# A retention layer and a feed-forward block on one core: five plain and three seven-product pairs in the first pass

## The chip, the cores and the metric

The kernel runs on one core of one Trainium2 chip. TensorE (PE) multiplies 128x128 weights with up to 512 columns; VectorE (DVE), ScalarE (ACT) and GpSimd (POOL) work on tiles of 128 partitions; SyncE (SP) issues all DMAs, in the order in which they are written. Each engine takes its own instructions in order and waits at semaphores for the others. The metric is the time of one execution on the device in microseconds.

## What is computed

```python
scores = (q @ k.T) / sqrt(64)                 # 8 batches, 8 heads, 576 tokens, 64 wide
ret = scores * where(i >= j, gamma[h] ** (i - j), 0)
x = (ret @ v)                                 # to 4608 tokens x 512
h = x @ w_in                                  # 512 x 2048
g = max(h, 0) + log1p(exp(-abs(h)))           # softplus
out = g @ w_out                               # 2048 x 512, fp32
```

The attention is computed in chunks of 128 tokens with a running state for each head. The feed-forward block takes most of the time.

## The kernel before

Every fp32 operand of the feed-forward block is split into a head (rounded to the matmul's fp32r) and a rest, and each product is the sum of three: rest x head, head x rest, head x head (`TERMS`). The tokens are nine units of 512; the hidden layer has 16 blocks of 128, two to a pair J (0 to 7).

Unit 0 goes through alone while the weights are loaded and split. The first pass does units 1 and 2. The three later passes do two units each, with seven products for each pair in both layers (`full_pair`, `full_phase`).

In the first pass most pairs are plain. A plain slot (`plain_slot`) makes one hidden block of one unit: two products of 6 matmuls into one bank (`acc` and `third` in turn), softplus (`size_of`, `log_of` on ACT; L486 on DVE), the split into head (ACT L490) and rest (DVE L494), and the 12 matmuls (L501) of the second layer for the block of the slot before. A slot's `jobs` are written behind that. The last pairs of the pass are made by `strassen_pair`: the four hidden blocks of a pair J, two of each unit, come from seven products in place of eight: B11, B21, T1, T2, B22, T3, NT4, in this order, into the banks `acc`, `two` and `third`. Their partial sums go to four quarters of two `quad` tiles: ACT copies a bank, DVE adds the next to it (L998, L1022, L1028). T2 adds to the bank from which ACT copies c[0] (L996), NT4 to the one that L1028 reads. Output matmuls of the pair before are spread between the products in quarters. The blocks of unit 2 are stored to DRAM (`kept_dram`) and fetched at the end of the pass (`kept_parts`).

A pair's seven products need sums of blocks: of the tokens (T1, T2, T3, NT4; `combined_x`, four subtractions for 128 tokens on POOL, then `finish_combined`: an ACT cast and a DVE subtraction) and of the weights. One set of weights' sums for one J is: whole (head + rest, two DVE additions, L634 or L649), four sums (L659 to L662), two heads (ACT L666), two rests (DVE L670), two stores of 512 KB. Input sums are for the pair's own seven products, output sums for the second layer in the later passes. Before, pairs are plain for J = 0 to 5 (`PLAIN = 6`); output set 0 is made in unit 1's slots, 1 and 2 in the two seven-product pairs, 3 and 4 in unit 2's slots, 5 to 7 in the next pass.

The order on each engine is the order of the code: nothing is moved afterwards. The table `jobs` says behind which slot a piece of work stands, `queued` is a list of DMA issues of which `product` takes one (two, where more than seven wait) behind each weight load. Weight blocks come through a ring of seven tiles, loaded seven products ahead. `quad` tiles are nine, in turn. An attention group (`chunk_products`) of one chunk stands in every second slot and in each seven-product pair, 13 in the first pass; its results leave the banks `two` and `third` through DVE (L244, L430, then the states L272, L273, L282 or L280).

Of the kernel before, what the change touches and what calls it, by code (L numbers as in the profile page):

```python
# [20 lines left out]
C = 128  # L21
NCHUNK = NTOK // C
NPAIR = H // 2
T = 512
# [31 lines left out]
PLAIN = 6  # L56
# [28 lines left out]
def retention_softplus_ffn(ctx: ExitStack, tc, first, whole, others, consts, w, out):  # L85
# [836 lines left out]
    def prepare_rest(j):  # L922
        combine_rest(raws[j])
# [25 lines left out]

    def start_combined(i, engine=nc.gpsimd):  # L950
        tmps[i] = quad().rearrange("p n (a b c) -> p (n a) b c", a=2, b=2)
        combined_x(tmps[i], column(i), engine)
# [4 lines left out]
    def schedule(*rows):  # L957
        plan = {}
        for p, f, *args in rows:
            plan.setdefault(p, []).append(lambda f=f, args=args: f(*args))  # L960
        return plan

    def half_b22(i):
# [5 lines left out]
        (1, prepare, PLAIN + 1), (1, prepare_whole, PLAIN), (2, prepare_sums, PLAIN), (3, prepare_split, PLAIN),  # L969
        (3, half_b22, 0), (4, prepare_store, PLAIN), (4, prepare_whole, PLAIN + 1), (4, prepare_sums, PLAIN + 1),  # L970
        (5, finish_combined, 0, nc.vector), (5, half_b22, 1), (6, prepare_split, PLAIN + 1),
        (6, prepare_ring, 4, 0, 3, 2), (7, prepare_store, PLAIN + 1), (7, prepare_ring, 4, 3, 4, 3),
        (7, finish_combined, 1, nc.vector), (7, half_b22, 2), (8, prepare_sums, 4), (9, prepare_ring, 5),
        (9, finish_combined, 2, nc.vector), (10, prepare_split, 4), (10, prepare_sums, 5), (10, half_b22, 3),
        (11, prepare_store, 4), (11, finish_combined, 3, nc.vector), (11, prepare_head, 5),
        (0, whole_out, 0), (1, combine_out, 0), (2, split_out, 0), (3, store_out, 0),
        *[(5 + 2 * j, raw_store, j) for j in range(4)])
    starts = schedule(*[(3 + 2 * i, start_combined, i) for i in range(CPU)])
    for p in range(2 * PLAIN):
        group = groups.pop() if p % 2 == 0 and p < 10 else None  # L980
        plain_slot(1, p, B11, B21, rest, group, (), *(x.get(p, ()) for x in (jobs, starts)))
# [6 lines left out]
    def strassen_pair(s, J, group, rest, last=False, extra=None):  # L988
# [12 lines left out]
        if extra is not None:  # L1001
            whole_out(extra)
        for j in stores:
            prepare_rest(j)
        if last:
            half_x(B12, STAGE[0, 1], slice(0, T), nc.gpsimd)
        ab = None if J == PLAIN else logs(c[0])
        output_some(-(-len(outputs) // 4))
        while stores:
            prepare_store(stores.pop(0))  # L1010
        product(z, T1, True)
        nc.scalar.copy(c[1], z)  # L1012
        ab = ab or logs(c[0])
        softplus(c[0], ab)
        if extra is not None:
            combine_out(extra)
        product(acc, T2)
        nc.scalar.copy(c[2], acc)
        if extra is not None:
            combine_head(raws["out", extra])  # L1020
# [10 lines left out]
        if extra is not None:  # L1031
            combine_rest(raws["out", extra])
# [33 lines left out]
        return [split_last, lambda: softplus_rest(gs[u1, 2 * J + 1], ab4)], kept  # L1066

    stores = [5]
# [7 lines left out]
    extras = {(0, NJ - 2): 1, (0, NJ - 1): 2}  # L1076
    for s in range(FULL):
        u2 = 2 + 2 * s
        first = PLAIN if s == 0 else 0
        more = s + 1 < NSUPER  # L1080
        for J in range(first, NJ):
            rest, kept = strassen_pair(s, J, groups.pop() if groups else None, rest, s == 0 and J == NJ - 1,
                                       extras.get((s, J)))
# [10 lines left out]
        if first:  # L1094
            blocks = schedule((0, prepare_ring, 0))
            plan = schedule(
                *[(2 * j - 1, prepare_ring, j) for j in range(1, 4)], *[(2 * j, prepare_sums, j) for j in range(4)],
                *[(2 * j + 1, prepare_split, j) for j in range(4)], *[(2 * j + 2, prepare_store, j) for j in range(4)],
                *[(8 + 2 * i, finish_combined, i, nc.vector) for i in range(2)],
                (9, half_x, B21, STAGE[1, 0], whole, nc.vector), *[(2 * j - 7, raw_store, j) for j in range(4, NJ)],  # L1100
                (4, whole_in, 3, 0), (6, combine_out, 3), (7, split_out, 3), (8, store_out, 3),
                (8, whole_in, 4, 1), (9, combine_out, 4), (10, split_out, 4), (11, store_out, 4))
            starts = schedule(*[(min(6 + 2 * i, 2 * first - 1), start_combined, i) for i in range(CPU)])
# [10 lines left out]
            job((0, 0), finish_combined, 2, nc.vector)  # L1114
            job((0, 1), half_x, B11, STAGE[0, 0], whole, nc.vector)
            job((1, 0), finish_combined, 3, nc.vector)
            job((1, 1), half_x, B22, STAGE[1, 1], whole, nc.vector)
# [302 lines left out]
```

## Time and profile before

| | us |
|---|---|
| median of 3 runs | 829.91 (829.48 to 829.99) |
| the profiled execution | 828.55 |
| its span, first to last instruction | 826.8 |
| PE busy | 814.9 (99%) |
| DVE busy | 642.9 (78%) |
| ACT busy | 546.7 (66%) |
| POOL busy | 165.7 (20%) |

A row of the timeline gives when an instruction (or several that follow each other) starts, how long it takes, its engine, line and tiles, and in brackets how long the engine stood idle before it and what released it. PE's matmuls overlap, so what a product takes is read from one start to the next. DVE's operations overlap a little, too: two of 512 columns that are shown as 1.28 us start 0.60 apart.

### The profile page before, as it was taken

How to read it: one execution, taken by the hardware profiler on the slowest of the kernel's cores; microseconds unless marked ns; L12 is line 12 of the kernel's file. 1: busy time of each engine (PE TensorE's matmuls, PEld its weight loads, DVE VectorE, ACT ScalarE, POOL GpSimd, SP SyncE). 2: the span in 40 equal slices, each digit the busy share in tenths (PEclk: the TensorE clock that was granted, in tenths of full speed). 3: DMA queues.
4: the chain of work that ended last, by engine and by line, in shares of the span. 5: the costliest groups of instructions: out<-in, count | busy, mean ns of one | idle time of the engine just before them, and what ended most of it. 6: DMA issues, size and time to landing. Idle time of an engine off the chain costs nothing.

```text
span 826.8 us, 19153 instructions
## 1 busy us (share of the span) xinstructions
PE 814.9 (99%) x7366; PEld 666.3 (81%) x7366; DVE 642.9 (78%) x1068; ACT 546.7 (66%) x957; POOL 165.7 (20%) x228
## 2 busy tenths in 40 slices
PE   8999999999999999999999999999999999999998
PEld 6788888888778888888887888888878888888886
DVE  5899987778787885778989995767889956555875
ACT  5787765546764554677877565776775658878643
POOL 3312221440221453111113000112110002212100
PEclk9999999999999999999999999999999999999999
DMA  9888979887789985598888678878757676666675
GB/s 355 315 296 293 321 238 368 291 290 256 260 288 354 314 301 171 198 304 267 276 259 283 218 213 258 256 226 267 227 166 215 216 245 192 193 194 192 191 216 173
DMA packets 149260, 209.95 MB, mean 254 GB/s; under 512 B 10801, under 2 KB 114737, under 8 KB 149169
## 3 DMA queue, kind: packets, MB, share of 16 engines
q1 hardware_dynamic: 149168, 208.72, 76.5%
q8 instruction: 59, 0.97, 0.5%
q14 instruction: 33, 0.26, 0.1%
HBM read 166.74 MB, written 41.94 MB: 252 GB/s over the span
## 4 chain that ended last, share of the span: by engine, by line
PE 88%; DVE 5%; ACT 4%; DMA 1%; issue 1%; SPq 0%; DVEq 0%; ACTq 0%
PE acc L855 20%; PE sum L1159 19%; PE y L501 14%; PE third L855 11%; PE two L855 4%; PE h L467 4%; PE two L1159 3%; PE acc L1159 2%; PE third L1159 2%; PE third L226 2%; PE two L288 1%; PE two L210 1%; PE two L300 1%; ACT ab L478 1%; ACT ab L479 1%
## 5 line engine op out<-in xcount | busy, mean ns | idle before, releaser
L855 PE MATMUL acc<-xt,ring 128*128 128x512 f32 x768 | 193.7, 390 | 0.9 <-DVE quad L1028 0.6
L1159 PE MATMUL sum<-parts,ring 128*128 128x512 f32 x720 | 174.0, 392 | 0.0
L855 PEld LDWEIGHTS acc<-xt,ring 128*128 128x128 f32 x768 | 143.5, 188 | 32.8 <-DVE quad L1028 1.0
L1149 ACT CAST parts<-g 128x512 fp32r<-128x512 f32 x168 | 102.8, 621 | 88.1 <-DVE g L1169 29.9
L1159 PEld LDWEIGHTS sum<-parts,ring 128*128 128x128 f32 x720 | 133.8, 188 | 28.6 <-DVE parts L1153 0.3
L1153 DVE TENSOR_TENSOR parts<-g,parts 128x512 fp32r<-128x512 f32 x168 | 118.0, 724 | 38.1 <-ACT parts L1149 36.1
L501 PE MATMUL y<-wout,g 128*128 128x512 f32 x576 | 140.1, 392 | 0.3 <-DVE g L494 0.3
L501 PEld LDWEIGHTS y<-wout,g 128*128 128x128 f32 x576 | 107.1, 188 | 23.3 <-PE h L467 0.7
L855 PE MATMUL third<-xt,ring 128*128 128x512 f32 x444 | 111.2, 390 | 0.0
L855 PEld LDWEIGHTS third<-xt,ring 128*128 128x128 f32 x444 | 83.2, 188 | 17.8 <-ACT quad L1012 0.3
L479 ACT ACTIVATE ab<-ab 128x512 f32<-128x512 f32 x120 | 75.9, 632 | 3.8
L478 ACT ACTIVATE ab<-ab 128x512 f32<-128x512 f32 x120 | 75.9, 633 | 3.5
L1169 DVE SCALAR_TENSOR_TENSOR g<-g,ab 128x512 f32<-128x512 f32 x96 | 67.1, 711 | 7.7 <-ACT ab L479 7.5
L203 POOL TENSOR_TENSOR qv<-qv,consts_sb 128x256 f32<-128x256 f32 x61 | 46.3, 758 | 106.2 <-DMA qv<-others 104.9
L490 ACT CAST g<-ab 128x512 fp32r<-128x512 f32 x44 | 27.3, 621 | 45.3 <-DVE ab L486 23.4
L467 PE MATMUL h<-xt,win 128*128 128x512 f32 x192 | 47.3, 395 | 1.1 <-DVE x L411 0.7
L284 POOL TENSOR_TENSOR s<-s,consts_sb 128x256 f32<-128x256 f32 (+1 forms) x31 | 20.3, 656 | 126.8 <-DVE s L282 109.5
L494 DVE TENSOR_TENSOR g<-ab,g 128x512 fp32r<-128x512 f32 x44 | 31.5, 716 | 18.3 <-ACT g L490 17.5
L474 ACT ACTIVATE ab<-g 128x512 f32<-128x512 f32 x72 | 45.0, 626 | 0.0
L1258 POOL TENSOR_TENSOR g<-g 128x512 f32<-128x512 f32 x10 | 14.1, 1408 | 149.1 <-DVE g L1169 149.1
L855 PE MATMUL two<-xt,ring 128*128 128x512 f32 x168 | 42.8, 391 | 0.8 <-DVE xs L430 0.8
L467 PEld LDWEIGHTS h<-xt,win 128*128 128x128 f32 x192 | 35.3, 188 | 9.2 <-DVE win L588 1.0
(193 smaller groups left out, 1339.6 us busy)
## 6 DMA issues: line engine op xcount, KB each, us to landing
ring<-split SPq DMA_DIRECT2D x126, 256.0 KB, 4.4
ring<-combined SPq DMA_DIRECT2D x104, 256.0 KB, 3.5
ring<-outcombined SPq DMA_DIRECT2D x96, 256.0 KB, 3.4
qv<-others SPq DMA_DIRECT2D x61, 320.0 KB, 4.6
ring<-outsplit SPq DMA_DIRECT2D x72, 256.0 KB, 3.5
wst<-w SPq DMA_DIRECT2D x32, 512.0 KB, 5.8
keys<-others SPq DMA_DIRECT2D x61, 256.0 KB, 4.6
split<-win SPq DMA_DIRECT2D x16, 512.0 KB, 6.3
```

Of the source, the lines that this page charges most:

```text
L203: nc.gpsimd.tensor_mul(v, v, f.unsqueeze(2).broadcast_to([P, 4, D]))
L467: nc.tensor.matmul(h, wins[p][:, a, kt * P:(kt + 1) * P], xt[:, b, T1 + kt // 2, kt % 2], start=(n == 0), stop=(n == 3 * NKT - 1))
L474: nc.scalar.activation(ab, h, AF.Abs)
L478: nc.scalar.activation(ab, ab, AF.Exp, scale=-1.0)
L479: nc.scalar.activation(ab, ab, AF.Ln, bias=1.0)
L494: nc.vector.tensor_sub(g[:, LO], ab, g[:, HI].bitcast(F32))
L501: nc.tensor.matmul(ys[u][tt], g[:, a, tt * P:(tt + 1) * P], wouts[p][:, b], start=(p == 0 and n == 0), stop=(p == NF - 1 and n == 2))
L855: nc.tensor.matmul(bank, w[:, ta, kt * P:(kt + 1) * P], xt[:, tb, x, kt], start=start and k == 0, stop=k == 5, skip_group_check=True)
L1149: nc.scalar.copy(t[:, HI], g_slot(J, n))
L1153: nc.vector.tensor_sub(t[:, LO], g_slot(J, n), t[:, HI].bitcast(F32))
L1159: nc.tensor.matmul(bank[m], w[:, a, m * P:(m + 1) * P], t[:, b], start=start and n == 0, stop=n == 2, skip_group_check=True)
L1169: nc.vector.scalar_tensor_tensor(c, c, 0.0, ab, op0=ALU.max, op1=ALU.add)
```

## The change

Pair 5 becomes a seven-product pair, so that there are five plain pairs and three others. The token sums are made by `start_wide` and `finish_wide`: 256 tokens at a time, in two halves, the subtractions on DVE. Pair 5 makes input set 7 ahead of its group and output set 1 behind it; pair 6 output sets 2 and 3; pair 7 output set 4. In a pair the first set's whole and sums stand behind the first addition, its heads behind the copy of c[2], its rests behind softplus of c[2]; the second set's whole, sums and heads stand behind the group, its rests in the next pair. The stores of both are put at the end of `queued`. Pair 7's B12 is subtracted on DVE, where it was POOL. Output sets 3 and 4 leave unit 2's slots, input set 4 is now made there and finished between the kept parts, of which there are six, where there were four.

```diff
-PLAIN = 6
+PLAIN = 5
+    def start_wide(i, half):
+        b11, b12, b21, b22 = (later["xs"][:, STAGE[n], :, wide(i)] for n in ((0, 0), (0, 1), (1, 0), (1, 1)))
+        t = quad().rearrange("p n (b c) -> p n b c", b=2)
+        if half == 0:
+            nc.vector.tensor_sub(t[:, 0], b12, b11)
+            nc.vector.tensor_sub(t[:, 1], b22, b12)
+        else:
+            nc.vector.tensor_sub(t[:, 0], b22, tmps[i, 0][:, 0])
+            nc.vector.tensor_sub(t[:, 1], b21, t[:, 0])
+        tmps[i, half] = t
+    def finish_wide(i, half):
+        at = slice(T1 + 2 * half, T1 + 2 * half + 2)
+        hi, lo = (xt[:, n, at, :, wide(i)] for n in (HI, LO))
+        t = tmps[i, half]
+        nc.scalar.copy(hi, t)
+        nc.vector.tensor_sub(lo, t, hi.bitcast(F32))
+    def in_sums(j):
+        return [lambda f=f: f(j) for f in (prepare_whole, prepare_sums, prepare_head, prepare_rest, prepare_store)]
+    def out_sums(j):
+        return [lambda: whole_out(j), lambda: combine_out(j), lambda: combine_head(raws["out", j]),
+                lambda: combine_rest(raws["out", j]), lambda: store_out(j)]
...
+        (9, finish_wide, 1, 0), (9, start_wide, 1, 1),
...
-        group = groups.pop() if p % 2 == 0 and p < 10 else None
+        group = groups.pop() if p % 2 == 0 else None
...
-    def strassen_pair(s, J, group, rest, last=False, extra=None):
+    def strassen_pair(s, J, group, rest, last=False, work=()):
...
-        if extra is not None:
-            whole_out(extra)
-        for j in stores:
-            prepare_rest(j)
+        for f in work[0][:2] if work else ():
+            f()
         if last:
-            half_x(B12, STAGE[0, 1], slice(0, T), nc.gpsimd)
-        ab = None if J == PLAIN else logs(c[0])
+            half_x(B12, STAGE[0, 1], slice(0, T), nc.vector)
         output_some(-(-len(outputs) // 4))
-        while stores:
-            prepare_store(stores.pop(0))
         product(z, T1, True)
         nc.scalar.copy(c[1], z)
-        ab = ab or logs(c[0])
+        ab = logs(c[0])
         softplus(c[0], ab)
-        if extra is not None:
-            combine_out(extra)
         product(acc, T2)
         nc.scalar.copy(c[2], acc)
-        if extra is not None:
-            combine_head(raws["out", extra])
+        for f in work[0][2:3] if work else ():
+            f()
...
-        if extra is not None:
-            combine_rest(raws["out", extra])
+        for fs in work[:1]:
+            fs[3]()
+            queued.append(fs[4])
...
-            if extra is not None:
-                combine_store(outs_dram[extra], raws.pop(("out", extra)))
             group_out(*group, between=(finish,))
+            for f in [x for fs in work[1:] for x in fs[:3]]:
+                f()
...
-        return [split_last, lambda: softplus_rest(gs[u1, 2 * J + 1], ab4)], kept
+        ends = [x for fs in work[1:] for x in (fs[3], lambda: queued.append(fs[4]))]
+        return [split_last, lambda: softplus_rest(gs[u1, 2 * J + 1], ab4)] + ends, kept
...
-    extras = {(0, NJ - 2): 1, (0, NJ - 1): 2}
+    work = {(0, PLAIN): (in_sums(PLAIN + 2), out_sums(1)), (0, PLAIN + 1): (out_sums(2), out_sums(3)),
+            (0, PLAIN + 2): (out_sums(4),)}
...
+        if s == 0:
+            rest = [lambda: None, lambda: finish_wide(1, 1), lambda: half_b22(3)]
...
+            job((0, 0), start_wide, 1, 1)
+            job((0, 0), half_x, B11, STAGE[0, 0], whole, nc.vector)
+            job((0, 1), finish_wide, 1, 0)
+            job((1, 0), finish_wide, 1, 1)
+            job((1, 1), prepare_rest, 4)
+            job((1, 1), prepare_store, 4)
+            job((2, 0), half_x, B22, STAGE[1, 1], whole, nc.vector)
```

Three places of the order. On ACT, from the logs of a pair's last block (L1037, now L1059, copies it from `acc`) to the copy of the next pair's first product from `acc` (L996, now L1024); before, between the two pairs:

```order
L1037 COPY quad<-acc 128x512
L474 ACTIVATE ab<-quad 128x512
L478 ACTIVATE ab<-ab 128x512
L479 ACTIVATE ab<-ab 128x512
L490 CAST g<-ab 128x512
L996 COPY quad<-acc 128x512
```

The same place of the change, between pairs 5 and 6:

```order
L1059 COPY quad<-acc 128x512
L474 ACTIVATE ab<-quad 128x512
L478 ACTIVATE ab<-ab 128x512
L479 ACTIVATE ab<-ab 128x512
L666 CAST quad<-quad 128x512 x2
L490 CAST g<-ab 128x512
L1024 COPY quad<-acc 128x512
```

The two heads of the second set (L666) have come between the logs and the split and copy.

On DVE, from the group's first result (L244) to the next pair's first addition (L998, now L1026) and on; before:

```order
L244 TENSOR_TENSOR a<-two,mask 128x512
L430 TENSOR_TENSOR xs<-two,consts_sb 128x4x128
L486 SCALAR_TENSOR_TENSOR ab<-quad,ab 128x512 x2
L280 COPY s<-third 128x256
L998 TENSOR_TENSOR quad<-two,quad 128x512
L494 TENSOR_TENSOR g<-ab,g 128x512
L649 TENSOR_TENSOR quad<-wout_183 128x512
L649 TENSOR_TENSOR quad<-wout_184 128x512
```

The same place of the change:

```order
L280 COPY s<-third 128x256
L649 TENSOR_TENSOR quad<-wout_181 128x512
L649 TENSOR_TENSOR quad<-wout_182 128x512
L659 TENSOR_TENSOR quad<-quad 128x256
L660 TENSOR_TENSOR quad<-quad 128x256
L661 TENSOR_TENSOR quad<-quad 128x256
L662 TENSOR_TENSOR quad<-quad 128x256
L1026 TENSOR_TENSOR quad<-two,quad 128x512
L494 TENSOR_TENSOR g<-ab,g 128x512
L670 TENSOR_TENSOR quad<-quad 128x512 x2
L649 TENSOR_TENSOR quad<-wout_183 128x512
L649 TENSOR_TENSOR quad<-wout_184 128x512
```

Output set 1 (weights 181 and 182) now stands ahead of the next pair's first addition, and set 2 follows behind it.

On DVE at the start of the first seven-product pair, behind the last slot's softplus; in the change (L970 is the subtraction of `finish_wide`, L961 and L962 the second half of `start_wide`):

```order
L494 TENSOR_TENSOR g<-ab,g 128x512
L970 TENSOR_TENSOR xt<-quad,xt 128x4x256
L961 TENSOR_TENSOR quad<-xs,quad 128x512
L962 TENSOR_TENSOR quad<-xs,quad 128x512
L1026 TENSOR_TENSOR quad<-two,quad 128x512
L970 TENSOR_TENSOR xt<-quad,xt 128x4x256
L438 TENSOR_TENSOR xt<-xs,xt 128x2x128
L634 TENSOR_TENSOR quad<-quad 128x512 x2
```

Before, that place held:

```order
L494 TENSOR_TENSOR g<-ab,g 128x512
L456 TENSOR_TENSOR xt<-quad,xt 128x8x128
L998 TENSOR_TENSOR quad<-two,quad 128x512
L649 TENSOR_TENSOR quad<-wout_181 128x512
L649 TENSOR_TENSOR quad<-wout_182 128x512
```

The second half of the token sums (the second L970, which T2 and NT4 read) now comes behind the pair's first addition.

## Rows read from the trace of the kernel before

**Rows 1.** The page, busy time and share of the span, by engine.

```profile
PE 814.9 (99%) x7366; PEld 666.3 (81%) x7366; DVE 642.9 (78%) x1068; ACT 546.7 (66%) x957; POOL 165.7 (20%) x228
```

**Rows 2.** Stretches: start:end, length, busy PE, PEld, DVE, ACT, POOL, clock, DMA.

```profile
118.00:196.40 78.40, 78.33 (x823) 64.68 (x822) 59.15 (x104) 41.43 (x73) 26.30 (x37) 1.00 0.86 296
196.40:230.70 34.30, 32.79 (x346) 25.64 (x344) 26.26 (x41) 25.36 (x43) 5.62 (x7) 1.00 0.81 278
230.70:306.00 75.30, 75.30 (x968) 62.36 (x972) 62.13 (x112) 40.24 (x72) 25.54 (x32) 1.00 0.93 327
```

**Rows 3.** The chain that ended last: start, us, what.

```profile
188.24 2.72 PE y L501 x12
196.40 1.36 PE acc L855 x6
199.12 0.68 PE y L501 x3
```

**Rows 4.** Timeline of PE in the two pairs: start, us, instruction, idle before.

```profile
196.24 1.52 PE L855 MATMUL acc<-xt,ring 128*128 128x512 f32 x6
...
207.21 1.65 PE L855 MATMUL acc<-xt,ring 128*128 128x512 f32 x6 [0.61 <-DVE quad L1028]
...
211.88 1.64 PE L855 MATMUL acc<-xt,ring 128*128 128x512 f32 x6
...
224.74 1.52 PE L855 MATMUL acc<-xt,ring 128*128 128x512 f32 x6
...
228.21 1.66 PE L501 MATMUL y<-wout,g 128*128 128x512 f32 x6
230.67 3.03 PE L855 MATMUL two<-xt,ring 128*128 128x512 f32 x12 [0.80 <-DVE xs L430]
```

**Rows 5.** Timeline of DVE there.

```profile
197.06 0.69 DVE L494 TENSOR_TENSOR g<-ab,g 128x512 fp32r<-128x512 f32 x1 [0.69 <-ACT g L490]
198.02 1.23 DVE L456 TENSOR_TENSOR xt<-quad,xt 128x1024 fp32r<-128x1024 f32 x1 [0.26 <-ACT xt L455]
...
200.14 1.28 DVE L649 TENSOR_TENSOR quad<-wout 128x512 f32<-128x512 f32 x2
...
204.28 0.42 DVE L659 TENSOR_TENSOR quad<-quad 128x256 f32<-128x256 f32 x1
...
205.87 0.68 DVE L1022 TENSOR_TENSOR quad<-third,quad 128x512 f32<-128x512 f32 x1
...
214.55 0.41 DVE L280 COPY s<-third 128x256 f32<-128x256 f32 x1
...
217.06 3.50 DVE L649 TENSOR_TENSOR quad<-wout 128x512 f32<-128x512 f32 x2
...
232.19 0.42 DVE L272 TENSOR_TENSOR u<-third,s 128x256 f32<-128x256 f32 x1
...
233.43 0.68 DVE L494 TENSOR_TENSOR g<-ab,g 128x512 fp32r<-128x512 f32 x1
```

**Rows 6.** Timeline of ACT there.

```profile
196.93 1.05 ACT L455 CAST xt<-quad 128x1024 fp32r<-128x1024 f32 x1
...
207.69 0.63 ACT L478 ACTIVATE ab<-ab 128x512 f32<-128x512 f32 x1
...
215.24 0.58 ACT L996 COPY quad<-acc 128x512 f32<-128x512 f32 x1
...
223.18 1.14 ACT L666 CAST quad<-quad 128x512 fp32r<-128x512 f32 x2 [3.29 <-DVE quad L662]
...
227.13 0.63 ACT L474 ACTIVATE ab<-quad 128x512 f32<-128x512 f32 x1 [0.44 <-DMA kept<-ab]
```

**Rows 7.** Timeline of POOL there.

```profile
216.84 2.56 POOL L438 TENSOR_TENSOR xt<-xs,xt 128x1024 fp32r<-128x1024 f32 x1 [1.12 <-ACT xt L435]
```

**Rows 8.** Timeline of SP, the issue of a store.

```profile
219.93 0.55 SPq L1042 DMA_DIRECT2D kept<-ab x1
```

**Rows 9.** DMA issues by line: count, KB each, median us to landing.

```profile
combined<-quad SPq DMA_DIRECT2D x16, 512.0 KB, 5.3
```

More of the change, by code (lines that the diff above doesn't have):

```diff
@@ L948, in retention_softplus_ffn, with wide @@
     tmps = {}
+    def wide(i):
+        return slice(2 * i * C, 2 * (i + 1) * C)
+    def start_wide(i, half):
[19 more added lines that the diff above has]
+                lambda: combine_rest(raws["out", j]), lambda: store_out(j)]
     def start_combined(i, engine=nc.gpsimd):
@@ L968, in retention_softplus_ffn @@
     jobs = schedule(
[L969 to L978, printed above, removed]
+        (0, whole_out, 0), (1, combine_out, 0), (1, prepare, PLAIN + 1), (1, prepare_whole, PLAIN), (2, split_out, 0),
+        (2, prepare_sums, PLAIN), (3, store_out, 0), (3, prepare_split, PLAIN), (3, half_b22, 0),
+        (4, prepare_store, PLAIN), (4, prepare_whole, PLAIN + 1), (5, prepare_sums, PLAIN + 1), (5, start_wide, 0, 0),
+        (5, half_b22, 1), (6, prepare_split, PLAIN + 1), (6, start_wide, 0, 1),
+        (7, prepare_store, PLAIN + 1), (7, finish_wide, 0, 0), (7, finish_wide, 0, 1),
+        (7, half_b22, 2), (8, prepare, PLAIN + 2), (8, start_wide, 1, 0),
+        (9, finish_wide, 1, 0), (9, start_wide, 1, 1),
+        *[(3 + 2 * j, raw_store, j) for j in range(4)])
+    starts = {}
     for p in range(2 * PLAIN):
-        group = groups.pop() if p % 2 == 0 and p < 10 else None
+        group = groups.pop() if p % 2 == 0 else None
         plain_slot(1, p, B11, B21, rest, group, (), *(x.get(p, ()) for x in (jobs, starts)))
@@ L1065, in split_last @@
             gs[u1, 2 * J + 1] = softplus_split(ab4)
-        return [split_last, lambda: softplus_rest(gs[u1, 2 * J + 1], ab4)], kept
-    stores = [5]
+        ends = [x for fs in work[1:] for x in (fs[3], lambda: queued.append(fs[4]))]
+        return [split_last, lambda: softplus_rest(gs[u1, 2 * J + 1], ab4)] + ends, kept
+    stores = []
     def kept_parts(u, J, g, n):
@@ L1080, in retention_softplus_ffn @@
         more = s + 1 < NSUPER
+        if s == 0:
+            rest = [lambda: None, lambda: finish_wide(1, 1), lambda: half_b22(3)]
         for J in range(first, NJ):
             rest, kept = strassen_pair(s, J, groups.pop() if groups else None, rest, s == 0 and J == NJ - 1,
-                                       extras.get((s, J)))
+                                       work.get((s, J), ()))
         for f in rest:
@@ L1096, in retention_softplus_ffn @@
             plan = schedule(
-                *[(2 * j - 1, prepare_ring, j) for j in range(1, 4)], *[(2 * j, prepare_sums, j) for j in range(4)],
+                *[(2 * j - 1, prepare_ring, j) for j in range(1, 5)], *[(2 * j, prepare_sums, j) for j in range(5)],
                 *[(2 * j + 1, prepare_split, j) for j in range(4)], *[(2 * j + 2, prepare_store, j) for j in range(4)],
[L1099 to L1103, printed above, removed]
+                (9, prepare_head, 4), (3, half_x, B21, STAGE[1, 0], whole, nc.vector),
+                (6, start_wide, 0, 0), (6, start_wide, 0, 1), (7, finish_wide, 0, 0), (8, finish_wide, 0, 1),
+                (9, start_wide, 1, 0), *[(2 * j - 7, raw_store, j) for j in range(4, NJ)])
+            starts = {}
             for p in range(2 * first):
@@ L1113, in retention_softplus_ffn @@
                 rest = []
[L1114 to L1117, printed above, removed]
+            job((0, 0), start_wide, 1, 1)
[5 more added lines that the diff above has]
+            job((2, 0), half_x, B22, STAGE[1, 1], whole, nc.vector)
         else:
```

## Prediction

> **What bounds the kernel now.** I read the page's first section, then the stretches of the first pass, then PE's own rows there, and last what DVE, ACT and POOL do beside it. TensorE is busy 814.9 of 826.8 us [rows 1]. In the first pass the plain slots of unit 1 (118 to 196.4 us) and of unit 2 (230.7 to 306 us) show it busy 78.33 of 78.40 and 75.30 of 75.30 us: nothing is to be had there but fewer matmuls. Only the two seven-product pairs have holes, 32.79 busy of 34.30 us [rows 2]. DVE is busy 26.26 of those 34.30 us, ACT 25.36.
>
> A product (6 matmuls) takes 1.36 us, a quarter of a block's outputs (3 matmuls) 0.68, a plain slot's 12 output matmuls 2.72 [rows 3]. The attention group in a pair takes 2.1 us with its edges: NT4's product starts at 224.74, so ends at 226.10, and the outputs start at 228.21 [rows 4]. A first pair (4 output quarters) is then 7 x 1.36 + 4 x 0.68 + 2.1 = 14.3 us of pure PE, any other (8 quarters) 17.1. Measured from start to start, 196.24 to 211.88 and 211.88 to 230.67 [rows 4], they take 15.64 and 18.79: 1.3 and 1.7 us lost, 3.0 together. Two of these waits are named, and both are DVE: 0.61 for L1028 (NT4 may not overwrite acc before it is added), 0.80 for L430 (the next slot needs the bank `two`).
>
> **One product less.** Pair J = 5 costs seven products instead of two slots in each unit with two each, so eight: -1.36 us. Outputs and groups stay the same in number (13 groups before and after). This is all that the change can give PE directly.
>
> **What the three pairs now hold.** I call them A, B, C (J = 5, 6, 7) and count in each from the start of its first product. Undisturbed PE: T2 starts at 4.76 in A and at 5.44 in B and C (two quarters precede T1 there, one in A). Prices: a DVE operation of 512 columns 0.60 from start to start, so two L649 or two L670 1.2 to 1.3; four sums 1.6 (204.28 to 205.87); the three states 1.24 (232.19 to 233.43); L456, now L970, 1.2 [rows 5]; on ACT two heads 1.1, one of three log steps 0.65 with the gap behind it, a copy 0.55 to 0.6, a cast of 1024 columns 1.05 [rows 6]. A set of sums on DVE is whole 1.2 + sums 1.6 + rests 1.3 = 4.1 us; there are five in three pairs now, and two in two before (with the rests of a third). DVE's own work in a pair is 11 operations x 0.60 + 1.24 = 7.8. So DVE needs 3 x 7.8 + 5 x 4.1 + 1.2 + 1.2 + 0.4 (finish_wide, B12, one block of B22) = 46.7 us, where PE has 14.3 + 17.1 + 17.1 = 48.5. No engine is over its time, but DVE is left 2 us in all, and what it does stands in one order.
>
> *Pair A.* T2 now needs the second half of finish_wide(1). In the last slot before, L494 stood at 197.06 and L456 at 198.02, so 0.8 and 1.8 to 3.0 after the pair's start at 196.24 [rows 5]; the same places hold L494 and the first L970. Then L961 and L962 to 4.2; only then can ACT cast (1.05, to 5.25), and L970 subtract (to 6.5). T2's first two matmuls read only the cast half and start at 5.3; the other four (0.91) at 6.5, end 7.4 instead of 6.12: 1.3 us. DVE follows with the block of B22 (0.35), whole and sums (to 9.7), softplus, L1043, L1049 at 11.7, where NT4 could have started at 11.5: 0.2. Pair A: 1.5 lost, 15.8 long. Bounds 0.5 (if the slot's own jobs run 1 us earlier) to 2.3 (the two L970 or the block of B22 late by what POOL's scaling beside them takes, some 0.8).
>
> *Pair B.* The second set of A is issued behind the group: DVE does L244, L430, two softplus, L280, then L649 twice and the four sums, and only then B's first addition L1026. ACT has the two heads of that set ahead of split_last and of the copy L1024 of acc. Before, L280 stood at 214.55, 2.7 after its pair's start, to 3.1 [rows 5], and nothing followed. Now whole to 4.2, sums to 5.7, heads to 6.85, split 7.4, copy 8.0. T2 adds into the very bank that this copy reads: it starts at 8.0 instead of 5.44, 2.55 us lost, with ACT and PE both idle on DVE. That ACT stands still like this when a head waits is a row of before: 3.29 us ahead of L666 at 223.18 [rows 6]. What is queued behind on ACT is all of B's softplus. On DVE L1026, the rests (to 10.5), whole and sums of the next set (to 13.3), softplus, L1043, L1049 at 15.15; T3 ended at 13.5 and two quarters later, 14.85, NT4 could start: 0.3. Pair B: 2.85 lost, 19.9 long. Bounds 1.8 (sums begin as soon as L280 ends and the copy follows the first head) to 4.5 (whole at 3.50, below).
>
> *Pair C.* After B's group DVE is later than after A's: ACT reaches the last log step at 21.5, softplus 22.15, three states instead of one copy, 23.4, so 3.5 in C's time; whole and sums to 6.3, heads 7.45, split 8.0, copy 8.55. T2 at 8.6: 3.15 lost. Then L1026, L494, rests to 11.1, whole and sums to 13.9, the subtraction of B12 that POOL did (1.2, to 15.1), softplus, L1043, L1049 at 16.9: NT4 waits 1.55. ACT's logs of c2 and c1 and DVE's rests put L430 at 22.6, where the next slot could begin at 21.7: 0.95. Pair C: 5.65 lost. Bounds 2.5 (as B, no drift) to 8.
>
> Weighed at this place: POOL. The two L649 that took 1.28 at 200.14 took 3.50 at 217.06, beside POOL's 2.56 us L438 that starts at 216.84 [rows 5, 7]. The change takes that POOL operation out of the pairs, so I use 1.28. The Trainium skill (GPSIMD Engine Reference, Key points) says that POOL shares its SBUF interfaces with VectorE and is in contention with DVE instructions that have two SBUF inputs; the trace agrees with it here, and by it the change has a gain that I do not count as time, since every later set in the pairs then costs 1.28. Were it 3.50 still, each later set would add 2.2 us.
>
> **The sum.** Lost in the pairs 1.5 + 2.85 + 5.65 = 10.0 us, before 3.0; with the product -1.36: +5.6 us. On the profiled execution, 828.55, that is 834.2. That execution lies 1.4 below the median of the runs, 829.91, so the forecast is 835.5.
>
> **At no cost.** POOL's sixteen subtractions a unit become eight DVE ones of 512 columns, 4.8 us; a slot of 5.44 us needs 1.2 of DVE by itself, and its outputs come a slot later, so 2 to 3 us of jobs fit. Sets 3 and 4 of the output sums leave unit 2's slots (8.2 us of DVE) and one input set and four subtractions come in: DVE stays at or under its 62.13 of 75.30 [rows 2]. Two more kept parts come after the slots with 2.72 us of PE each, six in all; DVE's work in them is 6 x 0.6 + 7.3 = 10.9 of 16.3 us. Without that cover either stage costs what it overruns, up to 1 us. SP: a store queued behind a load waits for its rest and lands 5.3 us later [rows 9]; set 7, whose rest is done at 15.9 in A, lands near 5.5 in B, when the load that reads it back is due; that load is used in C, ten microseconds on.
>
> **The rivals.**
> 1. Faster. The waits do not bind: DVE, without POOL beside it, reaches the second sets before L1026 needs it, and before's 0.80 at the slot goes too, since that came from the 3.50. Time: 829.91 - 1.36 - 0.8 = 827.7. For it: the 3.50 row. Against: the second set starts only when L280 ends, 3.1 in, and takes 2.8 us. It decides if the sums end before about 3 in B and C. Chance 0.08.
> 2. The drift does not add up: DVE uses PE's stall to catch up, and C loses what B does. 1.5 + 2.85 + 2.85 - 3.0 - 1.36 = +2.8: 832.7. For it: each T2 stall gives DVE 2.5 us. Against: DVE itself is what is stalled for. Chance 0.22.
> 3. Only the T2 waits in B and C, at their low bound (1.8 each), and A at 0.5: 4.1 - 3.0 - 1.36, about -0.3 to +1 with a stall left at the slot: 830.2, no change that can be told. Chance 0.10.
> 4. Longer: a log step waits for a kept store. One did, 0.44 us [rows 6]; such a store left at 219.93 and landed near 227.1, 7.2 us [rows 6, 8]. The store of c1 now leaves when the next pair's T2 is done, 10 in B, and lands at 17.2, when ACT wants its buffer at 17.1. Any later, and B and C grow by as much: +2, 837.5. Chance 0.12.
>
> The rest, 0.48, is the forecast itself, 833.5 to 837. A change under 0.2% (1.7 us) can't be told from none. Faster 0.08, same 0.10, slower 0.82. Eight times in ten I expect 830.5 to 837.6: the low end takes rivals 2 and 3 in, the high end rival 4.
>
> **What the profile after would show.** PE about 6 matmuls shorter. In B and C the T2 product on acc preceded by a wait of 2 to 3 us on ACT's L1024, ACT idle ahead of L666 on DVE's L662, and L1026 four to six microseconds after its pair's start. In A T2 split after two matmuls, on DVE's L970. In C NT4 late on L1049 and the first slot of unit 2 late on L430. DVE over 90% busy in the three pairs. Wrong would be: pairs of 14.3, 17.1 and 17.1 us, L666 without idle time ahead of it, or holes in the plain slots or in the kept parts.

## The result, and the profile after

The changed kernel took 836.9, 837.97 and 835.71 us; six later runs of it lay at 835.76 to 839.93, median 836.4. A fourth run beside the first three took 1639.31 us, in a slow state, and is left out of every comparison. Before took 829.95 (median of 4 beside it). The ratio is 1.0081, 95% interval 1.0067 to 1.0094: 5.6 to 7.8 us slower. 835.5 was forecast, 5.6 over before. The profiled execution, to which the rows below belong, is 836.9 long, 8.35 above that of before; some of that is chance, since the profiled run of before lay 1.4 under its median.

The page, busy time by engine (answers to [rows 1]):

```profile
PE 816.5 (98%) x7360; PEld 665.8 (80%) x7360; DVE 648.5 (78%) x1086; ACT 548.6 (66%) x960; POOL 135.6 (16%) x196
```

Six matmuls fewer, as forecast. PE's busy time rose all the same, by 1.6 us; the next views show where. Stretches of the first pass: unit 1's slots, pairs A, B and C, the first slots of unit 2 (columns as in [rows 2]):

```profile
118.00:185.10 67.10, 67.03 (x772) 55.33 (x772) 46.31 (x84) 34.07 (x61) 12.61 (x21) 1.00 0.96 334
185.10:201.70 16.60, 15.44 (x168) 11.81 (x167) 13.16 (x22) 12.59 (x21) 0.46 (x1) 1.00 0.59 199
201.70:222.90 21.20, 17.81 (x179) 14.07 (x178) 16.82 (x30) 12.96 (x24) 3.06 (x5) 1.00 0.78 267
222.90:245.90 23.00, 19.59 (x195) 15.06 (x193) 18.56 (x33) 14.03 (x25) 3.44 (x5) 0.93 0.73 249
245.90:312.00 66.10, 65.36 (x846) 54.12 (x847) 54.35 (x104) 33.59 (x59) 13.41 (x19) 1.00 0.96 331
```

Unit 1's slots are full, as before, and unit 2's have one hole of 0.7 us. The rest of the loss stands in the three pairs, and in C the granted clock is 0.93. PE's timeline there (answers to [rows 4]), with the two products behind T2 of C:

```profile
185.12 1.52 PE L855 MATMUL acc<-xt,ring 128*128 128x512 f32 x6
...
190.58 0.73 PE L855 MATMUL acc<-xt,ring 128*128 128x512 f32 x2 [0.54 <-ACT xt L969]
191.84 1.20 PE L855 MATMUL acc<-xt,ring 128*128 128x512 f32 x4 [0.53 <-DVE xt L970]
...
201.66 1.55 PE L855 MATMUL acc<-xt,ring 128*128 128x512 f32 x6
...
209.69 1.66 PE L855 MATMUL acc<-xt,ring 128*128 128x512 f32 x6 [2.38 <-ACT quad L1024]
...
217.81 1.66 PE L855 MATMUL acc<-xt,ring 128*128 128x512 f32 x6 [1.01 <-DVE quad L1049]
...
222.91 1.52 PE L855 MATMUL acc<-xt,ring 128*128 128x512 f32 x6
...
231.50 2.46 PE L855 MATMUL acc<-xt,ring 128*128 128x512 f32 x6 [3.00 <-ACT quad L1024]
233.76 2.35 PE L855 MATMUL third<-xt,ring 128*128 128x512 f32 x6
235.94 1.55 PE L501 MATMUL y<-wout,g 128*128 128x512 f32 x6
...
240.30 1.65 PE L855 MATMUL acc<-xt,ring 128*128 128x512 f32 x6
...
245.93 3.00 PE L855 MATMUL two<-xt,ring 128*128 128x512 f32 x12 [0.36 <-DVE xs L430]
...
255.47 0.27 PE L226 MATMUL third<-qv,keys 64*64 64x64 f32 x1 [0.70 <-POOL qv L203]
```

A hole is given below from the matmuls' starts: from the last start ahead of it, plus the 0.227 us of a matmul, to the next start. The bracket of a row counts from the end of the record, 0.16 later, so that B's hole of 2.55 shows as 2.38.

From start to start A takes 16.54, B 21.25, C 23.02 us: 2.2, 4.15 and 5.9 over the 14.3, 17.1 and 17.1 of pure PE, 12.3 where 10.0 was forecast and before lost 3.0 in two pairs. T2 starts 8.03 after its pair's start in B and 8.59 in C; 8.0 and 8.6 were forecast. Behind the hole of C the matmuls run at half speed: T2 takes 2.26 (231.50 to 233.76) and the next product 2.18, where 1.36 is usual. The clock granted there:

```profile
223.00:231.00 8.00, 5.51 (x25) 4.23 (x23) 6.08 (x12) 2.64 (x6) 0.93 (x1) 1.00 0.94 310
231.40:235.80 4.40, 4.30 (x12) 3.38 (x13) 4.28 (x7) 3.75 (x7) 1.54 (x2) 0.61 0.47 162
```

0.61 is a mean of TensorE's two levels: eight matmuls at 0.43 us (1.2 GHz), then 0.227 again (2.4 GHz). The eight lose 0.2 us each, 1.6 together, half of the 3.0 by which PE was busy beyond what six matmuls less would give. The other half stands in the pairs too: their busy time is 52.84 us, 4.3 over pure PE (1.6 of it the slow clock), where before's two had 32.79, 1.4 over. Each of the many holes adds to it, since the record of the last matmul ahead of one runs on into it.

What held T2, by ACT's and DVE's timelines (answers to [rows 6] and [rows 5]):

```profile
207.50 1.14 ACT L666 CAST quad<-quad 128x512 fp32r<-128x512 f32 x2 [4.43 <-DVE quad L662]
...
209.06 0.58 ACT L1024 COPY quad<-acc 128x512 f32<-128x512 f32 x1
...
229.31 1.14 ACT L666 CAST quad<-quad 128x512 fp32r<-128x512 f32 x2 [5.33 <-DVE quad L662]
...
230.88 0.58 ACT L1024 COPY quad<-acc 128x512 f32<-128x512 f32 x1
```

```profile
203.71 0.42 DVE L280 COPY s<-third 128x256 f32<-128x256 f32 x1
204.04 1.70 DVE L649 TENSOR_TENSOR quad<-wout 128x512 f32<-128x512 f32 x2
...
207.04 0.42 DVE L662 TENSOR_TENSOR quad<-quad 128x256 f32<-128x256 f32 x1
209.66 0.69 DVE L1026 TENSOR_TENSOR quad<-two,quad 128x512 f32<-128x512 f32 x1 [2.20 <-ACT quad L1024]
210.27 1.11 DVE L494 TENSOR_TENSOR g<-ab,g 128x512 fp32r<-128x512 f32 x1
...
212.52 1.73 DVE L649 TENSOR_TENSOR quad<-wout 128x512 f32<-128x512 f32 x2
```

The reader sees the ring of waits: DVE sums the second set, ACT stands 4.4 and 5.3 us for it with the copy of `acc` behind, PE stands for the copy, and then DVE itself stands 2.20 us for the copy. The two L649 take 1.70 and 1.73 where 1.28 was counted, and L494 1.11 where [rows 5] have 0.69. POOL's rows say what ran beside them (before, [rows 7]):

```profile
204.27 0.93 POOL L284 TENSOR_TENSOR s<-s,consts_sb 128x256 f32<-128x256 f32 x1 [2.75 <-DVE s L280]
210.23 0.62 POOL L203 TENSOR_TENSOR qv<-qv,consts_sb 128x256 f32<-128x256 f32 x1 [5.03 <-DMA qv<-others]
212.48 0.61 POOL L203 TENSOR_TENSOR qv<-qv,consts_sb 128x256 f32<-128x256 f32 x1 [1.63 <-DMA qv<-others]
```

SP at the end of C, two stores and the loads that the next group needs (answers to [rows 8]; the stores' time to landing in [rows 9], 5.3, is 5.5 now):

```profile
244.55 2.12 SPq L678 DMA_DIRECT2D outcombined<-quad  x2
246.76 0.70 SPq L162 DMA_DIRECT2D keys<-others  x1
247.55 1.15 SPq L168 DMA_DIRECT2D qv<-others  x1
```

### The profile page after: what moved, and what is told of

Its sections match the earlier page's. It is cut to its first block, busy times and chain, and to the rows that moved or that the text cites. A ratio compares the mean times of both kernels' runs of the same rounds, so it can differ in the third digit from the quotient of the medians.

```text
span 835.2 us, 19143 instructions
## 1 busy us (share of the span) xinstructions
PE 816.5 (98%) x7360; PEld 665.8 (80%) x7360; DVE 648.5 (78%) x1086; ACT 548.6 (66%) x960; POOL 135.6 (16%) x196
## 4 chain that ended last, share of the span: by engine, by line
PE 75%; DVE 11%; ACT 6%; DMA 5%; issue 2%; SPq 0%; POOL 0%; DVEq 0%; ACTq 0%; POOLq 0%
PE sum L1187 19%; PE acc L855 18%; PE third L855 10%; PE y L501 10%; PE two L855 4%; PE two L1187 3%; PE acc L1187 2%; PE third L1187 2%; PE third L226 2%; PE two L210 1%; ACT ab L478 1%; DMA split<-win 1%; DMA raw<-others 1%; PE two L288 1%; DMA wst<-w 1%
## 5 line engine op out<-in xcount | busy, mean ns | idle before, releaser
L855 PE MATMUL acc<-xt,ring 128*128 128x512 f32 x768 | 195.8, 392 | 7.6 <-ACT quad L1024 5.4
L855 PE MATMUL third<-xt,ring 128*128 128x512 f32 x432 | 109.2, 392 | 0.0
L203 POOL TENSOR_TENSOR qv<-qv,consts_sb 128x256 f32<-128x256 f32 x61 | 48.0, 787 | 113.0 <-DMA qv<-others 101.9
L284 POOL TENSOR_TENSOR s<-s,consts_sb 128x256 f32<-128x256 f32 (+1 forms) x31 | 21.0, 678 | 130.6 <-DVE s L282 114.3
L494 DVE TENSOR_TENSOR g<-ab,g 128x512 fp32r<-128x512 f32 x42 | 29.4, 699 | 16.5 <-ACT g L490 15.8
L855 PEld LDWEIGHTS two<-xt,ring 128*128 128x128 f32 x174 | 32.4, 188 | 7.9 <-DVE xs L430 1.2
```

The costliest lines, as they stand in the source:

```text
L203: nc.gpsimd.tensor_mul(v, v, f.unsqueeze(2).broadcast_to([P, 4, D]))
L494: nc.vector.tensor_sub(g[:, LO], ab, g[:, HI].bitcast(F32))
L855: nc.tensor.matmul(bank, w[:, ta, kt * P:(kt + 1) * P], xt[:, tb, x, kt], start=start and k == 0, stop=k == 5, skip_group_check=True)
```

## The experiments

Theory 1 was the forecast's: the second set's sums stand on DVE between a pair's group and its first addition, and its heads on ACT ahead of the copy that T2 needs. The rivals were that the pairs are long by something else, or that the sets cost wherever they stand. A loss given below is the time of the pairs from A's start to the next slot's start, less 48.5; the changed kernel's is 12.3.

**The second set's heads behind the next pair's first copy.**

```diff
-            for f in [x for fs in work[1:] for x in fs[:3]]:
+            for f in [x for fs in work[1:] for x in fs[:2]]:
-        ends = [x for fs in work[1:] for x in (fs[3], ...)]
+        ends = [x for fs in work[1:] for x in (fs[2], fs[3], ...)]
```

> The change with one edit: the two ACT heads (L666) of a pair's second set stand behind the next pair's copy of acc (L1024) in place of ahead of split_last and of that copy. All else, DVE's order too, is as in the change. Theory 1 (order on ACT): T2's waits of 2.4 and 3.0 us in pairs 6 and 7 go, and with the 3.0 us hole the stretch at a lower granted clock; some 0.6 us comes back ahead of B22, since the copy of c[1] now stands behind the heads. Pair 6 about 18.3 us (21.2 in the change), pair 7 about 19.5 (23.0), in all 830 to 831.5 us. Theory 2 (DVE is full, whatever ACT's order): the waits move to NT4 on L1049 and to the first slot on L430, and less than 2 us is won: 835 us or more.

833.75 (832.64 to 834.86), ratio to before 1.0046 (1.0030 to 1.0062): 3 us of the loss came back, which lies between the two theories (830 to 831.5, or 835 and more). The pairs take 56.34, a loss of 7.8, so 4.5 less; the group of slot 1 gave 0.9 of that back, as PE waited 1.6 us there for POOL's L203 (0.7 in the changed kernel). In B and C T2 no longer waits; the copy of the next bank does, since the heads that moved stand ahead of it on ACT, with a cast of 1024 columns. ACT and PE in C:

```profile
222.63 0.58 ACT L1024 COPY quad<-acc 128x512 f32<-128x512 f32 x1
226.62 1.14 ACT L666 CAST quad<-quad 128x512 fp32r<-128x512 f32 x2 [3.41 <-DVE quad L662]
227.67 1.04 ACT L435 CAST xt<-xs 128x1024 fp32r<-128x1024 f32 x1
228.61 0.58 ACT L1035 COPY quad<-third 128x512 f32<-128x512 f32 x1
```

```profile
229.24 1.66 PE L855 MATMUL third<-xt,ring 128*128 128x512 f32 x6 [2.07 <-ACT quad L1035]
```

So ACT's order was the near cause and DVE's order the one behind it.

**One set in a pair, the other two in unit 2's slots.**

```diff
-    work = {(0, PLAIN): (in_sums(PLAIN + 2), out_sums(1)), (0, PLAIN + 1): (out_sums(2), out_sums(3)),
-            (0, PLAIN + 2): (out_sums(4),)}
+    work = {(0, PLAIN): (in_sums(PLAIN + 2),), (0, PLAIN + 1): (out_sums(1),), (0, PLAIN + 2): (out_sums(2),)}
...
+                (4, whole_in, 3, 0), (6, combine_out, 3), (7, split_out, 3), (8, store_out, 3),
+                (8, whole_in, 4, 1), (9, combine_out, 4))
...
+            job((2, 0), split_out, 4)
+            job((2, 1), store_out, 4)
```

> The change with one set of sums in each pair: input set 7 in pair 5, output set 1 in pair 6, output set 2 in pair 7; output sets 3 and 4 are back in unit 2's slots (set 4 ends between the kept parts). Theory 1: no head stands ahead of a copy of acc any more, so T2 waits in pairs 6 and 7 are gone; these pairs lose about what the second pair lost before the change, 1.7 us each, pair 5 still its 1.7 on T2 and NT4; 830.5 to 832 us, if unit 2's slots hide two more sets on DVE. Theory 2 says the same for the pairs, so against e1 this tells how much of the loss is DVE's load: equal to e1 if order alone counts, 2 us or more below e1 if load counts.

831.95 (829.87 to 833.36), ratio 1.0023 (1.0011 to 1.0035). The pairs take 51.04, a loss of 2.5, all but nothing outside A: 5.3 less than with the heads alone moved, so what the second set does on DVE counts, and not its heads on ACT alone. But a late slot of unit 2 (0.8) and the kept parts behind it (0.6 and 1.2; the other 0.3 of the first line is in unit 0) now wait for DVE, which has two sets more to do there, and the time is only 1.8 shorter than with the heads moved:

```profile
PE y L501 <- DVE g L494: 2.1, 3, 1.2
...
PE third L855 <- DVE s L282: 0.8, 1, 0.8
```

**Both halves of the token sums before A.**

```diff
-        (7, half_b22, 2), (8, prepare, PLAIN + 2), (8, start_wide, 1, 0),
-        (9, finish_wide, 1, 0), (9, start_wide, 1, 1),
+        (7, half_b22, 2), (8, prepare, PLAIN + 2), (8, start_wide, 1, 0), (8, start_wide, 1, 1),
+        (9, finish_wide, 1, 0), (9, finish_wide, 1, 1),
...
-            rest = [lambda: None, lambda: finish_wide(1, 1), lambda: half_b22(3)]
+            rest = [lambda: None, lambda: half_b22(3)]
```

> The change with the second half of the token sums (start_wide(1, 1)) in slot 8, where DVE stood idle for 2.5 us, and finish_wide(1, 1) in slot 9, ahead of pair 5. Theory: T2 in pair 5 no longer splits on the ACT cast and DVE's L970, 0.54 + 0.53 us idle and 1.4 us in all are won, the rest is as in the change: 835.3 us where the change has 836.7. Rival: DVE is as late as before at L1049, and NT4 takes the wait over: under 0.5 us.

835.87 (834.9 to 836.35), ratio 1.0067 (1.0050 to 1.0085). A's two waits of 0.54 and 0.53 are gone and the pairs take 58.84, 2.0 less. In the time some 0.5 to 1 us of it shows, and with the intervals as they are that is no sure gain. Behind each of the holes that are left in B and C (2.25 and 2.82) there is a slow stretch in this trace.

**The heads' edit and the halves' together.**

> Both edits of e1 and e3 together. Theory 1: their gains add up (about 6 and 1.4 us): 828.5 to 830 us, so level with the kernel before or just under it. Theory 2: 833 us or more.

831.96 (829.07 to 833.93), ratio 1.0022 (0.9996 to 1.0049), again between the two theories; the pairs take 54.41.

**The same, with the last pair's store behind the next slots' loads.**

```diff
-            queued.append(fs[4])
+            if not last:
+                queued.append(fs[4])
...
+            if last:
+                queued.append(work[0][4])
```

> As e4_e1_e3, with one more thing: the store of the last pair's set 4 is issued behind the loads of the next slots' keys and queries. Theory 1 (the group of slot 1 waits since SP stands at that store, for DVE's L670, with the loads queued behind it): POOL's L203 in slot 1 no longer waits on the DMA of qv, and PE's wait there (0.5 us in e4, 0.7 in the changed kernel, 1.6 in e1) is gone; 831.3. Theory 2 (those loads are late by the traffic of the stores, not by SP's order): the wait stays, 832.

830.36 (829.15 to 831.38), ratio 0.9998 (0.9989 to 1.0007): as fast as before. PE's wait for POOL in slot 1 is gone: SP issues its second load of qv 0.7 us after the pairs' end, where it was 3.4, and POOL's second L203, which still waits 1.32 us for its load, ends 0.8 ahead of the group. SP's order had caused the wait. The step down from the kernel without it, 1.6 us, is more than the 0.5 that its trace shows for that wait, but the two intervals overlap.

**Sets 1 and 2 in unit 1's slots, the halves early, one set in a pair.**

```diff
...
-        (9, finish_wide, 1, 0), (9, start_wide, 1, 1),
+        (9, finish_wide, 1, 0), (9, finish_wide, 1, 1),
+        (3, whole_out, 1), (4, combine_out, 1), (6, split_out, 1), (7, store_out, 1),
+        (7, whole_out, 2), (8, combine_out, 2), (9, split_out, 2), (9, store_out, 2),
...
+    work = {(0, PLAIN): (in_sums(PLAIN + 2),), (0, PLAIN + 1): (out_sums(3),), (0, PLAIN + 2): (out_sums(4),)}
...
```

> Output sets 1 and 2 are summed in unit 1's plain slots, so that each pair holds one set; and both halves of the token sums for A are made in slots 8 and 9. Theory 1 (what was lost is DVE's time at the pairs' starts, by the queue of a second set; unit 1's slots have 46 of 67 us of DVE, so 8 us more hide there): no T2 wait on L1024 or on L969 and L970, holes in the pairs under 1.5 us together, and none in the slots; 828.4, that is before less the product of 1.36 us. Theory 2 (the pairs are slow by their own seven products, additions and copies, not by the sets): still two or more us of waits, 831.5 or more. Theory 3 (the sets cost wherever they stand, as DVE's waits moved to unit 2's late slots when the sets were put there): waits of 2 us or more in slots 6 to 9 of unit 1, 830.5.

828.74 (826.82 to 830.2), ratio 0.9980 (0.9968 to 0.9991): faster than before. B and C have no waits left, as theory 1 says. But theory 1 had holes of under 1.5 us in the three pairs together, and A alone, 17.47 long, loses 3.2. With the late store as well:

> As e6_sets_in_unit1, with the store of the last pair's set 4 behind the loads of the next slots. If that store holds the loads up in e6 as well: 0.5 us under e6, 827.9 where theory 1 holds. If one set in each pair leaves SP early enough: the same as e6.

827.44 (825.76 to 830.35), ratio 0.9968 (0.9956 to 0.9980), 1.7 to 3.7 us under before and the best of all; its interval overlaps that of the kernel without the late store. What the late store did there is open: without it, too, the group of slot 1 does not wait. The stretches of this best kernel are unit 1's slots, A up to its group, then that group with B, and C; below them is PE's first wait in A:

```profile
118.00:185.10 67.10, 67.03 (x772) 55.09 (x771) 52.20 (x96) 34.71 (x63) 12.69 (x20) 1.00 0.95 335
185.10:199.10 14.00, 13.10 (x52) 8.89 (x50) 11.54 (x20) 10.21 (x18) 0.78 (x2) 1.00 0.78 285
199.10:219.40 20.30, 20.30 (x295) 16.83 (x294) 15.25 (x27) 15.22 (x28) 3.16 (x6) 1.00 0.96 314
219.40:236.70 17.30, 17.30 (x196) 14.19 (x194) 13.92 (x24) 13.63 (x23) 2.54 (x5) 1.00 0.81 253
```

```profile
188.31 0.98 PE L501 MATMUL y<-wout,g 128*128 128x512 f32 x3 [0.36 <-DVE g L494]
```

DVE does 52.20 us in unit 1's slots where the changed kernel has 46.31, and PE still has no hole there; B and C are full (17.24 and 17.22, for 17.1). But A takes 17.11, a loss of 2.8, where it lost 0.6 with the halves early alone. Set 2's four sums stand on DVE ahead of the last slot's softplus, so that L494, for which A's first outputs wait, comes 2.5 us after A's start and not 0.8. The sets did cost something behind their new place, and theory 3 is right to that extent. In all the three pairs lose 3.1, as before's two lost 3.0, and what is left is the product: its profiled execution, 827.13, is 1.42 under that of before, for 1.36.

**Is the slow clock in C a cost of its own?** Three kernels put ten useless products ahead of T2 in B and C, so that TensorE works through the holes. The first wrote half of the bank `two`:

```diff
+        if work and J > PLAIN:
+            for n in range(10):
+                nc.tensor.matmul(two[:, 1], xt[:, HI, B11, 0, 0:P], xt[:, HI, B11, 1], ...)
         product(acc, T2)
```

> The changed kernel, with 10 useless products of 128x512 ahead of T2 in pairs B and C, into half of a bank that the next group overwrites, so that TensorE works in the holes of 2.4 and 3.0 us. Theory 1 (the slow matmuls behind the hole in C, at 1.2 GHz, come from TensorE having stood idle): no matmul runs at twice its time, T2 starts when it did, 1.5 us are won at most: 835.3, and the same as the changed kernel where that had no slow stretch. Theory 2 (the clock falls for another reason, or the fillers themselves run past L1024 and push T2): as slow as the changed kernel or slower, 836.7 to 838.

844.75 (842.54 to 847.79), ratio 1.0177: the experiment failed. The fillers waited for L1026 and L435, 3.14 and 3.33 us, came behind the holes, and themselves ran at 1.2 GHz, seven and eight of them. The second wrote the bank `third` (`z` in place of `two[:, 1]`), ahead of `product(z, T1, True)`:

> The changed kernel, with 10 useless products of 128x512 (2.27 us at 2.4 GHz) ahead of T1 in pairs B and C, into the bank of T1, which is free there: in e9_fillers they waited for L1026 and came behind the hole. Theory 1 (TensorE falls to 1.2 GHz behind the holes because it stood idle): the holes ahead of T2 shrink to 0.2 to 0.8 us, T2 starts when it did, no matmul runs at twice its time; 835.2, some 1.5 us under the changed kernel where that has one slow stretch, 3 where it has two. Theory 2 (the clock falls for another reason): slow matmuls as before; as slow as the changed kernel, or slower by what T1's later copy adds.

842.21 (841.91 to 843.56), ratio 1.0144. In B the fillers did as meant (0.28 us of hole left, clock 1.00); in C they waited 5.24 us for L435, and after that hole, the longest of all, eleven matmuls ran slowly.

The changed kernel again, beside it:

> The changed kernel once more, unchanged, beside e10_fillers_third on the same chip, since it had only three runs (836.9, 837.97, 835.71) and its slow stretches behind the holes may differ from execution to execution. By theory 1 of e10_fillers_third: 835.5 to 838, with a slow stretch behind at least one of the two holes of 2.4 and 3.0 us; the holes themselves the same to 0.1 us. By theory 2: the slow stretch elsewhere, or none.

836.37 (835.76 to 839.93), ratio 1.0070 (1.0049 to 1.0091). In its trace the holes are 2.55 and 3.15, the pairs 60.76, and the matmuls slow behind the second hole alone, as in the first trace. The third put the fillers ahead of `if last: half_x(B12, ...)` and the quarter of outputs:

> The changed kernel with the 10 useless products (2.27 us) one step earlier than in e10_fillers_third, ahead of the quarter of outputs before T1: there they wait for nothing but DVE's states, which are done. In e10 those of pair B filled the hole as meant (0.27 us left), those of pair C stood behind ACT's L435 and made a hole of 5.4 us. Theory 1 (TensorE falls to 1.2 GHz since it stood idle): holes ahead of T2 of 0.3 in B and 0.9 in C instead of 2.5 and 3.1, T2 as early as in the changed kernel, granted clock 1.00 in the pairs; 835, 1 to 1.5 us under the changed kernel. Theory 2 (the clock falls in pair C by something else there): slow products in C as before; 836.4, the same as the changed kernel.

838.38 (837.09 to 841.56), ratio 1.0098 (1.0080 to 1.0117). No matmul in the pairs is slow. Stretches of C: up to T2, and the 4.4 us that were slow in the changed kernel; then PE's rows for C's start, T2, NT4 and the next slot:

```profile
225.40:233.40 8.00, 7.84 (x34) 6.12 (x33) 6.17 (x12) 2.64 (x6) 1.00 (x2) 1.00 0.92 329
233.40:237.80 4.40, 4.19 (x18) 3.02 (x17) 3.82 (x6) 4.25 (x8) 1.49 (x2) 1.00 0.49 147
```

```profile
225.43 1.55 PE L855 MATMUL acc<-xt,ring 128*128 128x512 f32 x6
...
234.00 1.65 PE L855 MATMUL acc<-xt,ring 128*128 128x512 f32 x6 [0.21 <-ACT quad L1024]
...
242.80 1.65 PE L855 MATMUL acc<-xt,ring 128*128 128x512 f32 x6 [1.61 <-DVE quad L1053]
...
248.43 3.00 PE L855 MATMUL two<-xt,ring 128*128 128x512 f32 x12 [0.36 <-DVE xs L430]
```

With the holes filled the clock stayed up, so theory 1 holds in that. The other traces agree: of all fourteen, the five without a hole of 2 us in the pairs have no slow stretch there, and each of the nine slow stretches stands behind such a hole. But nothing was won. C takes 23.00 us, as with the slow clock (23.02), T2 stands 8.57 and NT4 17.37 after its start (8.59 and 17.39): what the matmuls no longer lose, NT4 waits for DVE (L1053 is the changed kernel's L1049). So the slow clock was free in C of the changed kernel, since DVE sets NT4's start. The whole run is 2 us longer than the changed kernel's, with intervals that overlap. The pairs, 60.77, do not hold that; the trace has small holes outside them that name no releaser, as the changed kernel's second trace has, and the cause stays open.

**POOL's small operations left out of the pairs.**

```diff
+        if heads.get("quiet"):
+            return
...
             nc.gpsimd.tensor_mul(v, v, ...)
...
+            if not heads.get("quiet"):
                 nc.gpsimd.tensor_mul(s, s, ...)
```

> The changed kernel without POOL's small multiplications (L203 and L284, 0.6 to 0.9 us each) in the three pairs: the scaling of the values and states of those groups is left out. Theory 1 (these stretch DVE's operations beside them: two L649 1.70 instead of 1.28, L494 1.11 instead of 0.69): two L649 take 1.28 in all three pairs, T2 in B and C comes 0.4 earlier each, the wait of NT4 in B falls from 1.2 to 0.3 or under, the first slot's group waits for the load itself; 834.5, 1.7 to 2 us under the changed kernel. Theory 2 (DVE's longer operations are longer for another reason, as DMA traffic): 1.70 as before, the same holes; 836.4.

This kernel leaves out the scaling of the values and states of those groups, so it serves for its rows alone. 834.5 (833.7 to 837.41), ratio 1.0061 (1.0042 to 1.0080), 1.9 under the changed kernel's 836.4; the intervals overlap, so the gain in time is not clear of noise. What POOL did to DVE is clear from the rows: first DVE in B (lines are three further on: L652 is L649, L1052 is L1049), then PE's T2 of B:

```profile
205.80 1.28 DVE L652 TENSOR_TENSOR quad<-wout 128x512 f32<-128x512 f32 x2
...
213.41 1.28 DVE L652 TENSOR_TENSOR quad<-wout 128x512 f32<-128x512 f32 x2
...
218.42 0.69 DVE L1052 TENSOR_TENSOR quad<-acc,quad 128x512 f32<-128x512 f32 x1 [0.81 <-PE acc L858]
```

```profile
211.02 2.55 PE L858 MATMUL acc<-xt,ring 128*128 128x512 f32 x6 [1.96 <-ACT quad L1027]
```

Two L649 take 1.28 each time, T2 in B and C waits 0.4 and 1.1 us less, and the pairs take 59.18, 1.6 less, nearly all of it in C (21.51 for 23.02). In B DVE is free for L1049 6.61 us after L1026 began (217.61, for 211.00), where it was 7.41. NT4 there starts without a wait, but the row of T2 says why: seven matmuls behind the hole of 2.12 ran slowly, so that DVE now stood 0.81 for PE. B takes 21.13, hardly less than 21.25. Here the slow clock was not free: it took what DVE had won.

## Why the prediction was right, and where its sizes were off

**The product**: 1.36 fewer, as forecast; the best kernel shows it by itself.

**T2 in B and C**: mechanism, place and size (2.55 and 3.15 forecast, 2.55 and 3.16 measured from the matmuls' starts). The sizes are a little lucky: two L649 took 0.42 more than counted, but the second set began 2.38 after B's start and 2.95 after C's, where 3.1 and 3.5 were counted. The heads moved, the sets moved out and POOL silenced each changed these waits as theory 1 says.

**A**: T2 was forecast 1.3 late, split after two matmuls, and was split in just that way, with two holes of 0.70; NT4 waited 0.27 for 0.2. Moving both halves forward took T2's wait away.

**NT4 in B**: 0.3 forecast, 1.17 measured. The step that was off is "the change takes that POOL operation out of the pairs, so I use 1.28". It takes out L438, but L284 and L203 of 0.6 to 0.9 us stayed, and two of them stretched L494 and two L649 by 0.42 and 0.45, which is the 0.87 missing. Without them DVE was 0.80 sooner at L1049. By the Trainium skill (GPSIMD Engine Reference, Key points) POOL and DVE contend where DVE reads two inputs from SBUF; the trace agrees, and also for operations of 0.6 us.

**C behind T2**: NT4 1.55 forecast. The changed kernel shows 0.26 of it as a wait and 1.6 as slow matmuls, and where the clock stayed up all of it is a wait on DVE, 1.77. The step held though its row was not the one foretold; the slow clock, which the forecast did not have, cost nothing at this place. The slot's start lost 0.53 for 0.95.

**The sum**: 12.3 lost for 10.0. 0.87 of the difference is NT4 in B, 0.17 the waits of A, 0.28 NT4 and the clock in C, less 0.42 at the slot; the other 1.4 is a fault of the sum. After each hole, and around each group, PE loses 0.09 to 0.14 us at a time (six matmuls behind a wait show as 1.65 or 1.66 where 1.52 is usual), 0.4 to 0.5 in a pair. The 3.0 that was subtracted for before, a measured difference, has these edges in it; the 10.0, built from named waits, has not. The group of slot 1 lost 0.7 more, unforeseen, since the store of set 4 stood ahead of its loads on SP. 12.3 + 0.7 - 3.0 - 1.36 is 8.6; the profiled executions differ by 8.35. That the medians differ by only 6.2 to 7.0, nearer to the 5.6 forecast, is partly luck: the trace of before, from which the sum was built, was a fast one.

**The rivals**: no drift (2) is refuted by C, 1.77 longer than B. A log step that waits for a kept store (4) did not occur: ACT has no such row in the pairs. Faster (1) and low bounds (3) are refuted by T2's rows. "DVE over 90% busy in the three pairs" was wrong, 79 to 81%: it stood 2.20 us in B and in C for the very copy that waited, through ACT, for it. The slots and kept parts have no holes, as foretold, but for the 0.7 in slot 1. "PE about 6 matmuls shorter" held for the count, not for its busy time.

## What to carry to other kernels

An engine with time to spare in all may have none at the place where work is put: ask what stands behind the new work in each queue, and who waits for that, and put it where the slack is (here unit 1's slots) rather than where there is room in the sum; then look at the end of that place, too, since what it finishes late (here set 2's sums, at A's start) is paid behind it. A wait that PE shows on one engine can be a second engine's order, so a fix of the near one only moves the wait to the next copy. When a loss is measured for before and summed from waits for after, count the edges on both sides.

## What the runs showed of the hardware

Behind some holes of TensorE the clock fell to 1.2 GHz, behind others of much the same length it did not. Ahead of T2: 2.55 us, no slow matmul (both traces of the changed kernel), 3.15 us, eight and seven; without POOL's operations 2.12 us, seven, and 2.06, none; with both halves early 2.25 and 2.82, eight and six; ahead of the late fillers 3.30, 3.50 and 5.40 us, seven, eight and eleven; where fillers left 0.28 to 0.37, none. Ahead of B22's product in C, with the heads moved: 2.23, none, 2.22 with the halves early as well, none, and the same 2.22 with the late store added, seven. What decides it for holes of 2.06 to 2.55 us the runs do not tell. Whether it costs time depends on what the next wait is: nothing in C of the changed kernel, where DVE came later still, and the whole gain in B without POOL's operations.

A small POOL operation (0.61 us alone) took 0.93 beside two of DVE's additions, while these took 1.70 for 1.28: both engines lose, each less than the other's whole operation.
